# Moving one early load to the GpSimd queue and one attention wave by one item in a lightning-attention and MLP kernel

## The chip, the core and the metric

The kernel runs on one core of a Trainium2 chip. A core has a tensor engine (PE) with its own weight loads (PEld), a vector engine (DVE), a scalar engine (ACT), GpSimd (POOL) and a sync engine (SP). They run side by side, each in its own program order, and wait for one another by semaphores. SP and POOL also issue the transfers between device memory and on-chip memory: SP's go through hardware queue q1, POOL's through software queue q0. The metric is the device time of one execution in microseconds (us); less is better.

## The reference

Linear attention with decay over 4 batches, 8 heads, 768 positions and head size 64, in blocks of 64 positions. Its output, laid out as 3072 tokens of 512 values, goes through an MLP with 2048 hidden values and the activation h · sigmoid(1.702 h).

```python
for b in range(nb):                                   # blocks of 64 positions
    intra = einsum('bhic,bhjc->bhij', qb, kb) * Dmask  # decay lam**(i-j), causal
    intra = einsum('bhij,bhjd->bhid', intra, vb)
    inter = einsum('bhid,bhde->bhie', qb * lam_pow, kv_state)
    out[:, :, sl] = intra + inter
    kv_state = lam_block * kv_state + einsum('bhsd,bhse->bhde', kb * rev_pow, vb)

x = out.transpose(0, 2, 1, 3).reshape(B * S, H * D)   # 3072 x 512
h = x @ w_in                                          # 512 -> 2048
g = h * (1.0 / (1.0 + exp(-1.702 * h)))
y = g @ w_out                                         # 2048 -> 512
```

## The kernel before, in words

**Waves.** The work is cut into six waves of 512 tokens. Waves 0 and 1 are of one kind: each holds two *halves* (c = 0, 1), and a half is the first 256 positions of one batch, two positions to a partition. Half c of wave w is batch 2w + c. Waves 2 to 5 hold 128 positions of all four batches each. The code calls c "batch" within a wave; "v of wave 0's batch 1" is `load_one(0, 1, "v", v)`.

**Attention of a half.** `do_cast` multiplies k and q by their decay powers and casts them to bf16 (on DVE or POOL); `turn_pe` transposes them on PE, and ACT or DVE copies the transposes out; `cast_v` casts v to bf16; `d_scores` makes the scores on PE and the masks on DVE; `d_one` and `d_state` make the state on PE from k and v; `d_out` multiplies masked scores with v, and `d_inter` adds the part from the state; `d_x` copies the result out as `xT`, the MLP's input. For wave 1 `start(1, c)` holds the scores and the first state, `end(1, c)` the outputs and the copies to `xT`. Waves 2 to 5 use `turn_dma`, a transpose by transfer issued on SP, and the functions `n_scores` to `n_out`.

**The MLP** is cut into items. `mlp1(w, fc)` is four matmuls of 512 columns (L393) with the activation on ACT; `mlp1_half(w, c, fc)` does two values of fc for the 256 columns of one half (eight matmuls of 256 columns, L405), so it needs only that half's `xT`. `mlp2(w, g, j)` is four matmuls of the second layer (L417), and the last of each g copies to `o_sb` on DVE (L421) and stores.

**The order is written out by hand.** The block from L457 to L512 is wave 0's start: casts, transposes, scores, outputs of its half 0, and the beginning of half 1. Between them stand *fillers* (`fill`, L143): matmuls on zeros whose result nobody reads. From L545 on, a main list holds all MLP items of all waves, and a side list holds attention steps, each with a place on the main list: a step at place n + 24 is issued just before main item 24 of that wave. `mlp_items` makes wave 0's list (31 items, indices 0 to 30: three half items, twelve `mlp1`, sixteen `mlp2`), and wave 1's starts at index 31. Because engines run in program order, a step that waits holds up all later instructions of its engine.

**The loads.** `load(0)` at L104 issues on SP k, q, v of half 0 (in two transfers each), then k and q of half 1 (two each), then v of half 1 in one transfer of 512 KB: eleven in all. The weights go through POOL and are converted from f32 to bf16 on the way: `w_in` in five parts (parts 0 and 1 of 256 KB, the others of 512 KB as written), `w_out` in four parts of 512 KB. POOL's order is: wait for v of half 0 (`gate_pool`, L472), issue w_in part 0, cast k of half 1 (four instructions, L198), issue w_in parts 1 and 2, cast half of v of half 1 (L211), issue w_in parts 3 and 4 and the four parts of w_out. SP's next instruction after `load(0)` is `gate_sync` (L506), a tiny transfer that reads w_out part 1; so SP issues `load(1)` only when that part has landed. Then come `load(2)`, the four transposes of wave 2 and the stores of wave 0.

**Where v of half 1 is used.** `cast_v(0, 1, (act_copy, pool_copy))` (L499) casts one part on ACT, one on POOL; then PE's `d_one(0, 1)` (L510) and `d_out` in `end(0, 1)` read it. On PE, `mlp1_half(0, 0, 0)` (L509), the first use of the weights, stands just ahead of `d_one(0, 1)`.

Of the kernel before, what the change touches and what calls it, by code (L numbers as in the profile page):

```python
# [24 lines left out]
def kernel(  # L25
# [13 lines left out]
    nc = tc.nc  # L39
# [36 lines left out]
    def load_one(w, c, nm, src):  # L76
        x = ld.tile([P, H, 2 * D], f32, tag=f"{nm}{c}", name=f"{nm}f")
        if w < ND:
            n = H if w or (nm == "v" and c) else H // 2
            for h in range(0, H, n):  # L80
                nc.sync.dma_start(  # L81
                    out=x[:, h : h + n],
                    in_=src[2 * w + c, h : h + n, 0 : 2 * P, :].rearrange("h (s a) d -> s h (a d)", a=2))
        else:
            nc.sync.dma_start(out=x.rearrange("p h (a d) -> p (h a) d", a=2),
                              in_=src[2 * c : 2 * c + 2, :, w * P : (w + 1) * P, :].rearrange("b h s d -> s (b h) d"))
        loaded[w, c, nm] = x

    def load(w, nms="kqv"):
        src = {"k": k, "q": q, "v": v}  # L90
        if w < ND:
            for c in range(HF):
                for nm in nms:
                    load_one(w, c, nm, src[nm])
        else:
            for nm in nms:
                for c in range(HF):
                    load_one(w, c, nm, src[nm])
# [3 lines left out]
    ones = const.tile([1, P], f32)  # L102
    nc.vector.memset(ones, 1.0)
    load(0)  # L104

    nc.scalar.preload_act_table_set("natural_log_exp_and_others")
# [29 lines left out]
    def acc(name, dt=f32, shape=None, tag="a"):  # L136
        return ps.tile(shape or [P, 4, P], dt, tag=tag, bufs={"a": 5, "mm": 3}[tag], name=name)

    def fill(n, new=None):
        if new:  # L140
            fill_ps[0] = acc("ps_fill", shape=[P, W], tag=new)
        for _ in range(n):
            nc.tensor.matmul(fill_ps[0], zero[:, 0:P], zero, start=True, stop=True)  # L143
# [31 lines left out]
    def load_w_in(j):  # L175
        c0 = sum(IN_CH[:j]) * P
        nc.gpsimd.dma_start(
            out=w_in_sb[j], in_=moe_w_in.rearrange("(kc ki) f -> ki kc f", ki=P)[:, :, c0 : c0 + IN_CH[j] * P])
# [10 lines left out]
    def do_cast(w, c, nm, eng, g=None):  # L189
        if g in (None, 0):  # L190
            cast[w, c, nm] = work.tile([P, 2, HD], bf16, tag=f"{nm}s{c}", name=f"{nm}s")
        f, x = loaded[w, c, nm], cast[w, c, nm]
        if w < ND:
            pw = {"k": kd_pow, "q": qd_pow}[nm]
            for R in (0, 1) if g is None else (g,):
                for j in range(2):
                    h = slice(4 * R + 2 * j, 4 * R + 2 * j + 2)
                    eng.tensor_tensor(x.rearrange("p a (r i j d) -> p r j i a d", i=2, j=2, d=D)[:, R, j],  # L198
                                      f[:, h].rearrange("p i (a d) -> p i a d", a=2),
                                      pw[:, h].unsqueeze(3).to_broadcast([P, 2, 2, D]), op=MUL)  # L200
        else:
            pw = {"k": k_pow, "q": q_pow}[nm]
            n = 2 * H // 4
            for j in range(2):
                eng.tensor_tensor(x.rearrange("p b (r i j d) -> p j (b r) i d", i=2, j=2, d=D)[:, j],  # L205
                                  f.rearrange("p h (a d) -> p (h a) d", a=2).rearrange("p (n j i) d -> p j n i d", j=2, i=2)[:, j],
                                  pw.rearrange("p b (r j i) -> p j (b r) i", i=2, j=2)[:, j].unsqueeze(3).to_broadcast([P, n, 2, D]),
                                  op=MUL)
# [19 lines left out]
    def turn_pe(w, c, nm, copy=act_copy, g=None):  # L228
        x = cast[w, c, nm]
        rr = list(range(NP)) if g is None else [2 * g, 2 * g + 1]  # L230
        t = acc("ps_t", bf16, [P, len(rr), 2, P])
        for i, r in enumerate(rr):
            for a in range(2):
                nc.tensor.transpose(t[:, i, a, :], x[:, a, r * P : (r + 1) * P], ident)  # L234
        if g in (None, 0):
            trans[w, c, nm] = work.tile([P, 2 * NP, P], bf16, tag=f"{nm}T{c}", name=f"{nm}T")
        copy(trans[w, c, nm][:, 2 * rr[0] : 2 * rr[0] + 2 * len(rr)], t.rearrange("p r a s -> p (r a) s"))
# [195 lines left out]

    def mlp_items(w):
        if w < ND:
            f = 4 if w == 0 else 8
            items = [(mlp1_half, w, c, fc) for c in range(HF) for fc in range(0, f, 2) if w or c or fc]
            items += [(mlp1, w, fc) for fc in range(f, FFC)]
        else:
            items = [(mlp1, w, fc) for fc in range(FFC)]  # L440
        if w == 0:
            items += [(mlp2, w, g, j) for j in range(NCH) for g in range(3)]
            return items + [(mlp2, w, 3, j) for j in range(NCH)]
        items += [(mlp2, w, g, j) for g in range(G) for j in range(NCH)]
        if w == NW - 1:
            items = items[:-NCH]
            for c0, c1 in ((0, 256), (256, 384), (384, 512)):
                items += [(mlp2, w, G - 1, j, c0, c1) for j in range(NCH)]
        return items

    def gate_pool(x):
        nc.gpsimd.tensor_copy(behind_q, x)
# [4 lines left out]
    with tc.manual_schedule():  # L457
# [4 lines left out]
            nc.scalar.activation(blk_pow[rows].rearrange("p (r i) -> p r i", i=2),  # L462
                                 ln_lam[rows].rearrange("p (r j i) -> p r j i", i=2, j=2)[:, :, j, :], EXP, scale=1.0 * P)
        nc.scalar.activation(warm, q_pow[:, 0, 0:1], GELU)
        fill(5)
        for nm, copies in (("k", (dve_copy, act_copy)), ("q", (act_copy, dve_copy))):
            for g in range(2):
                do_cast(0, 0, nm, nc.vector, g)
            for g in range(2):
                turn_pe(0, 0, nm, copies[g], g)  # L470
                fill(2 if nm == "k" or g == 0 else 0)
        gate_pool(loaded[0, 0, "v"][0:1, 0, 0:1])  # L472
        load_w_in(0)
        cast_v(0, 0, (act_copy, act_copy))
        d_scores(0, 0, 0)
        fill(1)
        d_scores(0, 0, 1)
        fill(3)
        for g in range(2):
            do_cast(0, 1, "k", nc.gpsimd, g)  # L480
        for j in (1, 2):
            load_w_in(j)
        d_one(0, 0, "mm")
# [18 lines left out]
        for j in range(NCH):  # L502
            load_w_out(j)
        nc.gpsimd.affine_select(mask, mask, pattern=[[0, 1], [1, P]], channel_multiplier=-1, base=0,
                                compare_op=mybir.AluOpType.is_ge, fill=0.0)
        gate_sync(w_out_sb[1][0:1, 0, 0:2])  # L506
        load(1)
        d_scores(0, 1, 1, True)
        mlp1_half(0, 0, 0)  # L509
# [36 lines left out]
        for w in range(NW):  # L546
            n = len(main)
            main += mlp_items(w)
            e = len(main)
            x = w + 1  # L550
            if x < ND:
                for c, (k_at, q_at, v_at, k_turn, q_turn, s_at, e_at) in enumerate(
                        ((19, 20, 19, 24, 25.5, 27, 30), (26.5, 28, 28, 29, 30, 32, 34))):
                    side += [(n + k_at, (do_cast, x, c, "k", (nc.vector, nc.gpsimd)[c])),
                             (n + q_at, (do_cast, x, c, "q", nc.vector)),
                             (n + v_at, (cast_v, x, c, ((pool_copy, pool_copy), (act_copy, act_copy))[c])),
                             (n + k_turn, (turn_pe, x, c, "k", act_copy)),
                             (n + q_turn, (turn_pe, x, c, "q", act_copy)),
                             (n + s_at, (start, x, c)), (n + e_at, (end, x, c))]
            elif x < NW:  # L560
                for c in range(HF):
                    tk, tq = (n + 2.1 + 2 * c, n + 4 + c) if x == ND else (n + 4 + 2 * c, n + 5 + 2 * c)
                    side += [(tk, (do_cast, x, c, "k", nc.vector)), (tk, (turn_dma, x, c, "k")),
                             (tq, (do_cast, x, c, "q", nc.vector)), (tq, (turn_dma, x, c, "q")),
                             (n + 10 + 2 * c, (cast_v, x, c, (dve_copy,)))]
                if x == ND:
                    side += [(n + 7, (stores,))]
                t = n + 16
                side += [(t, (n_two, x, 0)), (t + 4, (n_two, x, 1)), (t + 9, (n_rest, x))]
            if w + 2 < NW:  # L570
                side += [(n + (12 if w else 20), (load, w + 2))]
# [36 lines left out]
```

## Time and profile before

| | us |
|---|---|
| six runs | 207.19, 208.25, 208.55, 209.45, 209.83, 209.97 |
| median | 209.0 |
| the profiled execution | 209.97 |
| its span in the profile | 208.2 |

All times below are from the start of that span. The transfers of the first 45 us, from the profile's transfer lists and the chain of waits:

| transfer | issued on | issued at | landed at |
|---|---|---|---|
| k of half 0, two parts | SP | 0.81, 1.33 | 3.6, 4.2 |
| q of half 0, two parts | SP | 1.85, 2.40 | 6.4, 6.9 |
| v of half 0, two parts | SP | 2.95, 3.50 | 7.9, 8.6 |
| k of half 1, two parts | SP | 4.16, 5.59 | 9.9, 11.3 |
| q of half 1, two parts | SP | 6.32, 7.01 | 11.3, 12.1 |
| v of half 1 | SP | 7.97 | 16.60 |
| w_in part 0 | POOL | 8.26 | 16.29 |
| w_in part 1 | POOL | 12.23 | 17.9 |
| w_in part 2 | POOL | 12.98 | 21.7 |
| w_in parts 3, 4 | POOL | 17.2, 18.0 | 24.7, 27.3 |
| w_out parts 0, 1 | POOL | 18.7, 19.4 | 30.0, 32.53 |
| k, q, v of wave 1, half 0 | SP | 33.35, 33.78, 34.40 | 39.16, 40.7, 42.2 |

What PE did at those places: 5.83 first transposes of half 0; 9.10 and 9.77 its two score groups; 10.87 `d_one(0, 0)`; 11.24 first transposes of half 1; 14.97 end of half 1's scores; 16.30 `mlp1_half(0, 0, 0)`; 17.29 `d_one(0, 1)`; 19.38 main item 0; 22.06 first use of w_in part 2; 32.42 first `mlp2`; 40.0 to 40.2 the transposes of wave 1's k; 50.7 wave 1's first MLP item; 66.67 scores of wave 2; 205.3 last matmul.

How to read the profile: a line of the timeline gives the start, the length, the engine, the source line, the operation with output and inputs, how many instructions it merges, and in brackets how long the engine was idle before it and what it then waited for. A line of the chain of waits gives the start, the length and what held up the chain there. A row of busy time gives the sum, the share of the span and the number of instructions.

### The profile page before, as it was taken

Reading aid. Unit: us, or ns where it says so; the run is one execution under the profiler, and the core shown is the slowest. Engines: PE = TensorE matmul, PEld = TensorE weight load, DVE = VectorE, ACT = ScalarE, POOL = GpSimd, SP = SyncE. Lnnn points to the kernel's source line nnn. Section 1 sums busy time; section 2 is a strip of 40 time slices with the busy share of each in tenths; the row PEclk is TensorE's granted clock in tenths of the full one; section 3 lists DMA queues with packets and bytes.
Section 4 is the critical chain, followed back from the end, with each engine's and each line's share of the span. In section 5 each row is a group of like instructions: output and inputs, shape, how many; then the busy total and the mean of one; then the engine's idle time right before and its main releaser. Section 6 shows DMA issues by size and latency. Waiting matters only on the chain.

```text
span 208.2 us, 4271 instructions
## 1 busy us (share of the span) xinstructions
PE 199.5 (96%) x1806; PEld 105.3 (51%) x1830; DVE 89.4 (43%) x160; ACT 86.3 (41%) x158; POOL 16.4 (8%) x37
## 2 busy tenths in 40 slices
PE   7988999999999999999999999999999999999994
PEld 2556544457864454444464444464444454444453
DVE  1793000486970844750744750744750741100121
ACT  4866662148666012466012466012466012566000
POOL 4368200060000000000000000000000000000000
PEclk9999999999999999999999999999999999999999
DMA  5999999999999899989992379991360021100112
GB/s 150 328 221 155 184 202 219 284 324 228 231 210 163 199 247 231 263 193 211 212 257 104 93 167 213 238 252 52 99 154 3 14 90 50 50 0 0 54 50 101
DMA packets 87640, 33.82 MB, mean 162 GB/s; under 512 B 67398, under 2 KB 84678, under 8 KB 87622
## 3 DMA queue, kind: packets, MB, share of 16 engines
q1 hardware_dynamic: 82868, 29.37, 56.7%
q0 software_dynamic: 4752, 4.19, 13.0%
q8 instruction: 14, 0.23, 0.4%
q14 instruction: 4, 0.03, 0.0%
q10 hardware_dynamic: 2, 0.00, 0.0%
HBM read 27.26 MB, written 6.29 MB: 161 GB/s over the span
## 4 chain that ended last, share of the span: by engine, by line
PE 75%; DMA 15%; SPq 4%; DVE 2%; POOL 1%; issue 1%
PE ps_out L417 35%; PE ps_h L393 28%; DMA w_out<-in_moe_w_out_dram 6%; DMA vf<-in_v_dram 4%; PE ps_h L405 3%; SPq L81 3%; DMA kf<-in_k_dram 3%; PE ps_s L331 2%; DMA qT<-qs 2%; PE ps_o L381 2%; PE ps_o L368 1%; DVE o_sb L421 1%; PE ps_t L234 1%; PE ps_kv L355 1%; DVE ks L198 1%
## 5 line engine op out<-in xcount | busy, mean ns | idle before, releaser
L417 PE MATMUL ps_out<-w_out,g_sb 128*128 128x512 bf16 (+2 forms) x400 | 83.8, 362 | 1.1 <-issue 0.6
L393 PE MATMUL ps_h<-xT,w_in 128*128 128x512 bf16 x330 | 73.2, 379 | 0.3
L395 ACT ACTIVATE g_sb<-ps_h 128x512 bf16<-128x512 f32 x84 | 50.2, 597 | 45.2 <-PE ps_h L393 45.2
L417 PEld LDWEIGHTS <-g_sb 128*128 128x128 bf16 x416 | 38.2, 98 | 41.0
L393 PEld LDWEIGHTS <-w_in 128*128 128x128 bf16 x336 | 32.9, 98 | 39.2
L421 DVE COPY o_sb<-ps_out 128x512 f32<-128x512 f32 (+2 forms) x26 | 16.9, 650 | 52.4 <-PE ps_out L417 52.3
L339 DVE SCALAR_TENSOR_TENSOR sm<-ps_s,inv_pow,mask 128x512 bf16<-128x512 f32 x32 | 21.8, 743 | 28.1 <-PE ps_s L331 28.1
L385 ACT CAST xT<-ps_o 128x512 bf16<-128x512 f32 x16 | 8.2, 599 | 38.3 <-PE ps_o L381 38.3
L405 PE MATMUL ps_h<-xT,w_in 128*128 128x256 bf16 x96 | 11.4, 273 | 1.3 <-DMA w_in<-in_moe_w_in_dram 1.3
L198 DVE TENSOR_TENSOR ks<-kf,kd_pow 128x256 bf16<-128x256 f32 x8 | 2.9, 421 | 22.2 <-DMA kf<-in_k_dram 18.9
L405 PEld LDWEIGHTS <-w_in 128*128 128x128 bf16 x96 | 9.0, 98 | 3.1 <-DMA w_in<-in_moe_w_in_dram 1.5
L205 DVE TENSOR_TENSOR qs<-qf,q_pow 128x512 bf16<-128x512 f32 x16 | 10.3, 685 | 0.0
L205 DVE TENSOR_TENSOR ks<-kf,k_pow 128x512 bf16<-128x512 f32 x16 | 10.3, 684 | 0.0
L263 DVE TENSOR_TENSOR sm<-ps_s,mask_d 128x512 bf16<-128x512 f32 x14 | 8.8, 684 | 0.8 <-PE ps_s L255 0.5
L407 ACT ACTIVATE g_sb<-ps_h 128x512 bf16<-128x512 f32 x12 | 7.2, 598 | 4.3 <-PE ps_h L405 4.3
L143 PE MATMUL ps_fill<-zero 128*128 128x512 bf16 x18 | 7.3, 536 | 1.4 <-DVE zero L113 1.4
L359 DVE SCALAR_TENSOR_TENSOR kv<-kv,blk_pow,ps_kv 128x256 bf16<-128x256 bf16 x12 | 5.0, 475 | 6.0 <-PE ps_kv L355 6.0
L217 ACT COPY kT<-ps_t 128x512 bf16<-128x512 bf16 (+1 forms) x4 | 3.2, 797 | 8.4 <-PE ps_t L234 8.4
L198 DVE TENSOR_TENSOR qs<-qf,qd_pow 128x256 bf16<-128x256 f32 x16 | 5.8, 425 | 0.1
L214 DVE CAST v_sb<-vf 128x1024 bf16<-128x1024 f32 x8 | 5.2, 687 | 0.8 <-DMA vf<-in_v_dram 0.8
L331 PEld LDWEIGHTS <-kT 64*128 64x128 bf16 x128 | 3.6, 94 | 3.9 <-issue 3.9
L331 PE MATMUL ps_s<-qT,kT 64*128 64x128 bf16 x128 | 5.1, 217 | 0.3 <-DMA qT<-qs 0.3
(68 smaller groups left out, 91.9 us busy)
## 6 DMA issues: line engine op xcount, KB each, us to landing
vf<-in_v_dram SPq DMA_DIRECT2D x11, 512.0 KB, 6.8
kf<-in_k_dram SPq DMA_DIRECT2D x10, 512.0 KB, 5.7
qf<-in_q_dram SPq DMA_DIRECT2D x10, 512.0 KB, 6.9
out_dram<-o_sb SPq DMA_DIRECT2D x15, 256.0 KB, 2.0
out_dram<-o_sb SPq DMA_DIRECT2D x17, 128.0 KB, 2.4
w_out<-in_moe_w_out_dram POOLq DMA_DIRECT2D x4, 512.0 KB, 14.0
w_in<-in_moe_w_in_dram POOLq DMA_DIRECT2D x3, 512.0 KB, 8.7
kf<-in_k_dram SPq DMA_DIRECT2D x4, 256.0 KB, 3.0
```

What stands on the lines that cost most here:

```text
L143: nc.tensor.matmul(fill_ps[0], zero[:, 0:P], zero, start=True, stop=True)
L198: eng.tensor_tensor(x.rearrange("p a (r i j d) -> p r j i a d", i=2, j=2, d=D)[:, R, j], f[:, h].rearrange("p i (a d) -> p i a d", a=2), p ...
L205: eng.tensor_tensor(x.rearrange("p b (r i j d) -> p j (b r) i d", i=2, j=2, d=D)[:, j], f.rearrange("p h (a d) -> p (h a) d", a=2).rearran ...
L263: nc.vector.tensor_tensor(sm.rearrange("p i a s -> p i (a s)"), flat, mask_d.rearrange("p o a b s -> p o (a b s)").to_broadcast([P, 2, 2 * ...
L331: nc.tensor.matmul(s2[h][:, b, :], kT[hs, (b % 2) * NP + p, :], qT[hs, (b % 2) * NP + p, :], start=True, stop=True)
L339: nc.vector.scalar_tensor_tensor(sm, s, inv_pow[:, n : n + 1], mask.to_broadcast([P, B, P]), op0=MUL, op1=MUL)
L385: nc.scalar.copy(xT[w][:, p, :], ps_o.rearrange("p b s -> p (b s)"))
L393: nc.tensor.matmul(h, w_in_sb[j][:, kc, i * P : (i + 1) * P], xT[w][:, kc, :], start=(kc == 0), stop=(kc == KC - 1))
L395: nc.scalar.activation(g_of[w][:, fc, :], h, GELU)
L405: nc.tensor.matmul(h[:, u, :], w_in_sb[j][:, kc, i * P : (i + 1) * P], xT[w][:, kc, cols], start=(kc == 0), stop=(kc == KC - 1))
L417: nc.tensor.matmul(ps_out, g_of[w][:, fc, g * P : (g + 1) * P], w_out_sb[j][:, fc % CW, c0:c1], start=(fc == 0), stop=(fc == FFC - 1))
L421: nc.vector.tensor_copy(o, ps_out)
```

## The change

1. `load_one` issues v of wave 0's half 1 on POOL (`nc.gpsimd`), and `load(0)` leaves it out. It is issued where the new line `load_one(0, 1, "v", v)` stands, in POOL's order behind w_in part 0 and the four casts of k, ahead of w_in parts 1 and 2.
2. Five fillers go: the first group has three for five; behind the four transpose groups stand 2, 1, 1, 0 for 2, 2, 2, 0; and the one between the two score groups is taken out.
3. All of wave 1's attention steps stand one main item later.
4. Wave 1's list of MLP items begins with five half items for each half (fc 0 to 9), then six `mlp1`; before it was four and eight.

```diff
@@ load_one
-                nc.sync.dma_start(
+                (nc.gpsimd if w == 0 and c and nm == "v" else nc.sync).dma_start(
@@ load
-                    load_one(w, c, nm, src[nm])
+                    if w or c == 0 or nm != "v":
+                        load_one(w, c, nm, src[nm])
@@ mlp_items
-            f = 4 if w == 0 else 8
+            f = 4 if w == 0 else 10
@@ start of wave 0
-        fill(5)
+        fill(3)
...
                 turn_pe(0, 0, nm, copies[g], g)
-                fill(2 if nm == "k" or g == 0 else 0)
+                fill(2 - g if nm == "k" else 1 - g)
...
         d_scores(0, 0, 0)
-        fill(1)
         d_scores(0, 0, 1)
         fill(3)
         for g in range(2):
             do_cast(0, 1, "k", nc.gpsimd, g)
+        load_one(0, 1, "v", v)
         for j in (1, 2):
             load_w_in(j)
@@ side list of wave 1
                 for c, (k_at, q_at, v_at, k_turn, q_turn, s_at, e_at) in enumerate(
-                        ((19, 20, 19, 24, 25.5, 27, 30), (26.5, 28, 28, 29, 30, 32, 34))):
+                        ((20, 21, 20, 25, 26.5, 28, 31), (27.5, 29, 29, 30, 31, 33, 35))):
```

## The prediction, made before the changed kernel was run

> **What bounds the kernel now.** I read the page first: PE is busy 199.5 of 208.2 us, so the gaps on PE are 8.7 us in all. Two of the page's lines show how little else is near the limit.
>
> ```profile
> PE 199.5 (96%) x1806; PEld 105.3 (51%) x1830; DVE 89.4 (43%) x160; ACT 86.3 (41%) x158; POOL 16.4 (8%) x37
> PEclk9999999999999999999999999999999999999999
> ```
>
> The gaps lie almost wholly in the first 20 us, and the waits list gives PE only two of any size after its first instruction. The chain of waits, in order of time, then shows something that PE's business hides: up to 39 us, and once more at 67 us, a chain of transfers sets the pace.
>
> ```profile
> 7.97 8.62 DMA vf<-in_v_dram
> 16.60 0.06 issue
> 16.66 0.61 POOL v_sb L211
> 17.26 1.44 POOL w_in L177 x2
> 18.70 0.72 POOL w_out L181
> 19.42 13.09 DMA w_out<-in_moe_w_out_dram
> 32.53 0.77 SPq L455
> 33.35 5.81 DMA kf<-in_k_dram
> 39.19 1.45 DVE ks L198 x4
> ...
> 62.90 4.38 DMA qT<-qs
> 67.31 0.51 PE ps_s L331 x12
> ```
>
> SP has nothing to do until w_out's second part lands at 32.53 (its longest wait, 23.3 us); from 33.35 it issues loads of waves 1 and 2 without a gap until 57.4, then four transposes. The last lands at 67.28, and PE has waited for it since 66.96. So there are two clocks: PE's own work, and the transfers through w_out's gate. They meet at 67.3 with PE 0.35 us ahead. Behind that point PE waits for nothing but 0.05 to 0.2 us of issue. **A gain before 67.3 reaches the end only if both clocks gain.**
>
> The timeline gives the place that the change touches:
>
> ```profile
> 9.96 2.32 POOL L198 TENSOR_TENSOR ks<-kf,kd_pow 128x256 bf16<-128x256 f32 x4 [0.76 <-DMA kf<-in_k_dram]
> 12.23 1.55 POOL L177 DMA_DIRECT2D w_in<-in_moe_w_in_dram  x2
> 16.30 1.05 PE L405 MATMUL ps_h<-xT,w_in 128*128 128x256 bf16 x8 [1.33 <-DMA w_in<-in_moe_w_in_dram]
> 16.62 0.62 ACT L217 CAST v_sb<-vf 128x512 bf16<-128x512 f32 x1 [1.37 <-DMA vf<-in_v_dram]
> 16.66 0.61 POOL L211 CAST v_sb<-vf 128x512 bf16<-128x512 f32 x1 [2.87 <-DMA vf<-in_v_dram]
> 67.31 0.51 PE L331 MATMUL ps_s<-qT,kT 64*128 64x128 bf16 x12 [0.35 <-DMA qT<-qs]
> ```
>
> PE waits 1.33 us for the first weights (landed 16.29), and v of batch 1 lands only 0.31 us later (16.60). Behind v stand both casts, then PE's d_one at 17.29.
>
> [...] from 12.5 to 13.0 us POOL's queue moved 96 packets and SP's 100. So moving v takes no byte away; it only changes the order. [...] fillers come 0.43 us apart to 7 us and 0.21 us later. [...] the w_in issues at 12.23 beside DVE's casts took 0.75 us, the w_out issues beside an idle DVE 0.77.
>
> **The change, part by part.**
>
> *Fillers.* Five of twenty go. Two of the first five end at 5.4 instead of 5.83; the first cast halves are ready at 4.63 + 2 x 0.36 = 5.35, so transposes start 0.4 us earlier. The rest brings the second scores from 9.77 to about 9.15 (they then wait for qT). But the next transposes, at 11.24, need POOL's first two casts, done at 9.96 + 2 x 0.61 = 11.17: up to there the gain is zero. Behind it DVE's masks end 0.46 us earlier, and the scores of batch 1 end near 14.5 instead of 14.97. All this only makes the wait for weights or v longer: worth 0 at the end. [...]
>
> *First weights.* They are issued at 8.26 in both kernels. By half microseconds POOL's queue moves its first packets at 11.0 to 11.5, when SP's k and q of batch 1 run out (2.62 MB at some 330 GB/s). Without v beside them, 528 packets at 166 a half microsecond (14.5 to 15.0, nearly alone) take 1.6 us: they land at 13.5 to 14.5 instead of 16.29. PE starts them at 14.5, not 16.30.
>
> *v of batch 1.* Now issued on POOL behind its four casts, at 12.28 instead of SP's 7.97. Until the first packet: w_in's fourth part was issued at 17.21 and its packets came at about 19.2, so 2.0 us; between 1.2 (the queue was already busy) and 2.7 [...]. Transfer: 1,024 packets at SP's 345 a half microsecond are 1.5 us, at w_in's 166 they are 3.1; I take 1.8, nearer to SP's[...]. End of landing: 0.4 us (k's first halves, with no backlog, 0.3 to 0.5). Sum: 12.28 + 2.0 + 1.8 + 0.4 = **16.5**, bounds 15.4 and 18.6. Before it was 16.60. So PE gains **0.1 us** (bounds +1.2 and -2.0) at d_one; the wait of 1.33 us for weights becomes one for v. Queued behind v: on ACT the copy of a score tile (0.58) and on DVE its mask (0.43), which hold PE's d_out, as before; on POOL all of w_in's last parts and w_out.
>
> *Weights behind v.* w_in's second part is issued up to 1.5 us later and runs behind v: 16.1 + 1.6 + a tail of 0.5 to 1.2 = 18.2 to 18.9, needed at 19.3: covered. The third: 2.65 us more, 21 to 22, needed at 22: just covered, up to 0.3 us exposed. [...]
>
> *The gate.* Before, POOL's queue nearly ran dry at 18.0 to 20.0: 81, 39, 50 and 78 packets a half microsecond where 98 is usual, 144 missing, 0.73 us. With v in the same queue two weight parts still stand in line when POOL goes on, so that dip goes; a new one opens between the first weights' end (12.9) and v's first packet (14.3), 1.4 us. The mean loses 0.7, but landings came 2.0 us behind the mean (third w_in: mean 19.6, landed 21.7), and an idle 1.4 us lets the laggards catch up. I take 32.53 - 0.3, bounds -1.2 and +1.5.
>
> *One item later, half-wave items.* No work is added but two pairs as halves: 16 matmuls at 0.112 us (L405, 40 in 4.47) for 8 at 0.220 (L393, 41 in 9.01), +0.03 us. Wave 1's transposes stand 0.87 us later in PE's order (four L417 matmuls), so PE comes at 40.77 and finds k cast (40.3): the 0.27 us wait there goes. All other steps of wave 1 get 0.87 us more slack. One cover goes: the last output item no longer lies between end(1,0) and the first half-wave item, and its o_sb copy (0.69) now precedes the xT copy on DVE. DVE ends xT about 1.75 us after d_out begins, PE's d_out, states and eight transposes take 1.7: 0 to 0.15 us, I take 0.1. Wave 2's casts follow 0.8 us later on DVE; SP took them 1.7 to 3.1 us after they were ready, so nothing waits.
>
> *Sum.* PE reaches the scores of wave 2 at 66.96 - 0.1 + 0.03 + 0.1 = 67.0; qT lands at 67.28 - 0.3 = 67.0. So PE goes on 0.3 us earlier. The profiled execution took 209.97 us (span 208.2 and 1.8 around it) and becomes 209.7; it was the slowest of six, so against the median, 209.0, I forecast **208.7**.
>
> **Rivals.** *Both clocks gain:* POOL's queue starts v at once and runs at SP's rate: v 15.4, gate -1.2. PE would be 1.2 + 0.35 - 0.13 = 1.4 us earlier, transfers 1.2: 207.8. For it: the queue is busy when v is issued; against: w_in's first part needed 3 us. *Only one gains:* v lands at 15.5, but the gate stays; PE stands 1.3 us longer at the wave-2 scores: 209.0. For it: SP's gapless chain. This holds too if v merely changes places with the weights, so that the change does not do what it says. *Slower:* v, late on POOL's queue. Its price is one for one once v lands later than 16.60 + 0.35 - 0.13 = 16.8, the point where PE falls behind qT. At 18.6 PE is 1.8 us late: 210.8; PE then idles from 15.5 to 19.3[...]. [...]
>
> **How the numbers follow.** Forecast 0.45, its own range 208.2 to 209.2; both clocks gain 0.13; only one 0.17; slower 0.25, of which somewhat under half passes 1%. One per cent (2.1 us) is about what a measurement can tell here, as the runs of before differ by 2.8. Faster by over 1% needs more than the best bounds give and is left 0.05; slower by over 1% gets 0.11; within 0.84. Range 207.5 to 210.6.
>
> **What would show it.** First weights landed by 14.5 and no PE wait for them; a PE wait for v_sb instead; v issued near 12.3 and landed by 16.8; no dip of POOL's packets at 18 to 20; w_out's gate at 31.3 to 33; PE waiting under 0.2 us at wave 1's transposes; the wave-2 scores within 0.5 us of 67. Wrong: v past 17.5, L405 matmuls at twice their length, or a new wait for w_in.

## The result, and the profile after

The changed kernel took 210.39 us (median of 35 runs, 208.88 to 212.53) where the kernel before, run beside it, took 208.35 (72 runs, 206.96 to 212.07). The ratio is 1.0087, with a 95% interval of 1.0066 to 1.0107: slower, by more than the measurement is uncertain. Ratios here leave out the executions that lie over 1.5% above the fastest of their kernel, so they are not the plain quotients of the medians. The forecast had been a small gain, 209.0 to 208.7.

The profiled execution took 209.47 us, span 207.8; the profiled execution before 209.97, span 208.2. Profile against profile, the change gained 0.5 us (forecast: 0.3), while the medians lost 2.0. Most of what follows is about that contradiction.

From the page of the changed kernel, the row of busy time and the row of POOL's DMA queue (packets, MB, share of 16 engines):

```profile
PE 198.4 (95%) x1811; PEld 105.1 (51%) x1833; DVE 89.5 (43%) x160; ACT 86.3 (42%) x158; POOL 17.1 (8%) x38
q0 software_dynamic: 4896, 4.72, 14.1%
```

PE is busy 198.4 of 207.8 us, so the gaps are now 9.4 us (8.7 before). v moved to POOL's queue adds only 144 packets and 0.53 MB to the 4,752 and 4.19 MB before: v's packets there carry about 4 KB each, and are not the 1,024 small ones of my estimate.

The waits of PE (total, times, longest):

```profile
PE ps_kv L276 <- ACT v_sb L218: 1.5, 1, 1.5
```

The wait for the first weights has gone, and the one for v stands in its place (1.5 us for 1.33). The chain of waits shows the same (start, length, what held it):

```profile
4.17 5.57 DMA kf<-in_k_dram
9.89 2.27 POOL ks L199 x4
12.16 4.48 DMA vf<-in_v_dram
...
19.49 2.77 PE ps_h L406 x24
```

v is now behind POOL's four casts: they end at 12.16, v takes 4.48 us from there, and behind its landing PE is the chain up to the end. The gate of w_out and the transfers of wave 1 have left the chain. From the timeline:

```profile
12.16 0.95 POOL L81 DMA_DIRECT2D vf<-in_v_dram  x1
14.82 1.05 PE L406 MATMUL ps_h<-xT,w_in 128*128 128x256 bf16 x8
16.70 0.61 POOL L212 CAST v_sb<-vf 128x512 bf16<-128x512 f32 x1 [2.08 <-DMA vf<-in_v_dram]
17.34 0.38 PE L276 MATMUL ps_kv<-v_sb,ks 64*64 64x64 bf16 x13 [1.47 <-ACT v_sb L218]
19.42 2.84 PE L406 MATMUL ps_h<-xT,w_in 128*128 128x256 bf16 x24
66.54 0.74 PE L332 MATMUL ps_s<-qT,kT 64*128 64x128 bf16 x16
```

PE starts the first weights at 14.82 without a wait, ends them at 15.87 and stands until 17.34. d_one(0, 1) and main item 0 begin at 17.34 and 19.42: the same places as in the profile before (17.29, 19.38). So against that profile nothing is lost; the question is what that profile stands for.

### The profile page after: what moved, and what is told of

The parts are those of the page before. It is cut to its first block, busy times and chain, and to the rows that moved or that the text cites. A ratio compares the mean times of both kernels' runs of the same rounds, so it can differ in the third digit from the quotient of the medians.

```text
span 207.8 us, 4280 instructions
## 1 busy us (share of the span) xinstructions
PE 198.4 (95%) x1811; PEld 105.1 (51%) x1833; DVE 89.5 (43%) x160; ACT 86.3 (42%) x158; POOL 17.1 (8%) x38
## 4 chain that ended last, share of the span: by engine, by line
PE 88%; DMA 5%; SPq 1%; DVE 1%; issue 1%; POOL 1%; ACT 1%; ACTq 0%; POOLq 0%
PE ps_out L418 39%; PE ps_h L394 34%; PE ps_h L406 6%; DMA kf<-in_k_dram 3%; PE ps_s L332 2%; DMA vf<-in_v_dram 2%; PE ps_o L382 2%; SPq L81 1%; PE ps_o L369 1%; DVE o_sb L422 1%; POOL ks L199 1%; PE ps_t L235 1%; PE ps_o L313 1%; PE ps_kv L356 1%; PE ps_o L295 1%
## 5 line engine op out<-in xcount | busy, mean ns | idle before, releaser
L394 PE MATMUL ps_h<-xT,w_in 128*128 128x512 bf16 x322 | 71.5, 379 | 0.3
L394 PEld LDWEIGHTS <-w_in 128*128 128x128 bf16 x328 | 32.1, 98 | 38.2
L406 PE MATMUL ps_h<-xT,w_in 128*128 128x256 bf16 x112 | 13.1, 273 | 0.0
L199 DVE TENSOR_TENSOR ks<-kf,kd_pow 128x256 bf16<-128x256 f32 x8 | 2.9, 420 | 22.6 <-DMA kf<-in_k_dram 19.3
L406 PEld LDWEIGHTS <-w_in 128*128 128x128 bf16 x112 | 10.5, 98 | 1.7 <-DVE xT L215 0.2
L144 PE MATMUL ps_fill<-zero 128*128 128x512 bf16 x14 | 6.1, 539 | 1.5 <-DVE zero L114 1.4
```

The costliest lines, as they stand in the source:

```text
L394: nc.tensor.matmul(h, w_in_sb[j][:, kc, i * P : (i + 1) * P], xT[w][:, kc, :], start=(kc == 0), stop=(kc == KC - 1))
L406: nc.tensor.matmul(h[:, u, :], w_in_sb[j][:, kc, i * P : (i + 1) * P], xT[w][:, kc, cols], start=(kc == 0), stop=(kc == KC - 1))
```

## The experiments

The expectations weigh three theories. *Late v*: v lands later than it mostly does on SP, and PE waits for it. *Clock*: the changed kernel falls more often into a short stretch at half the TensorE clock. Of its executions 16 have a mean clock of 0.992, over spans of about 209 us; at half clock that is a stretch of 3.3 us, worth 1.7 (an estimate from these clocks). The one profile that shows such a stretch (e9) has 3.4 us of it, at 0.50. *Order*: wave 1's new order costs time.

Each row was timed beside the kernel before on the same chip. The last column counts timed executions whose mean granted TensorE clock was below 0.995.

| Run | Median us | Ratio, 95% | Below 0.995 |
|---|---|---|---|
| kernel before, again | 208.01 | 0.9995 [0.9966, 1.0024] | 6 of 22 |
| changed kernel | 210.39 | 1.0087 [1.0066, 1.0107] | 21 of 36 |
| v alone (e1) | 210.03 | 1.0073 [1.0047, 1.0100] | 6 of 17 |
| fewer fillers alone (e2) | 208.60 | 1.0009 [0.9984, 1.0034] | 0 of 22 |
| wave 1's order alone (e7) | 208.20 | 0.9981 [0.9957, 1.0004] | 1 of 22 |
| all but v's move (e6) | 208.06 | 1.0001 [0.9973, 1.0028] | 0 of 22 |
| changed, six fillers in the wait (e3) | 209.23 | 1.0052 [1.0032, 1.0072] | 0 of 22 |
| changed, four fewer fillers (e8) | 209.99 | 1.0078 [1.0052, 1.0104] | 12 of 20 |
| changed, v ahead of the casts (e5) | 208.53 | 0.9997 [0.9967, 1.0027] | 1 of 14 |
| before, v ahead of the casts, wave 1's order (e10) | 208.79 | 1.0002 [0.9979, 1.0025] | 0 of 22 |

The changed kernel's 36 are its 35 timed executions and the profiled one. The kernel before itself was below 0.995 in 19 of 164 executions beside these runs.

### The kernel before, again

No edit.

> The kernel before, once more, for the granted clock and the span of each execution, which are known for the changed kernel only: there 15 executions at clock 0.998 to 1.0 had a median of 209.28 us, 17 at 0.991 to 0.992 had 210.82, and 4 at 0.984 had 212.21. Clock theory (what is lost is a stretch of about 3.4 us at half clock, worth some 1.6 us, that the changed kernel falls into more often): before shows the same steps, but most executions at 1.0, with the 207.5 us that are its commonest time belonging to 1.0. Order theory (wave 1's new order costs time at full clock): before at clock 1.0 is 1 to 2 us faster than the changed kernel at 1.0. Late-v theory: the clock is the same in both, and the times differ without it.

The profiled execution took 207.8 us, 2.2 less than the profile that I had predicted from. Its timeline (SPq is SP's DMA issue):

```profile
7.94 0.69 SPq L81 DMA_DIRECT2D vf<-in_v_dram  x1
14.19 0.61 POOL L211 CAST v_sb<-vf 128x512 bf16<-128x512 f32 x1 [0.91 <-DMA vf<-in_v_dram]
14.76 1.05 PE L405 MATMUL ps_h<-xT,w_in 128*128 128x256 bf16 x8 [0.30 <-ACT sm L261]
15.73 0.37 PE L275 MATMUL ps_kv<-v_sb,ks 64*64 64x64 bf16 x12
17.68 2.84 PE L405 MATMUL ps_h<-xT,w_in 128*128 128x256 bf16 x24
30.89 0.77 SPq L455 DMA_DIRECT2D behind<-w_out  x1
65.04 0.62 PE L331 MATMUL ps_s<-qT,kT 64*128 64x128 bf16 x16
```

Here v, issued at 7.94 for 7.97, lands before 14.2, and not at 16.60; the first weights cost no wait for a transfer either. Everything behind it is earlier: d_one(0, 1) at 15.73, not 17.29; the gate at 30.89, not 32.53; wave 2's scores at 65.04 with no wait for qT, not 66.67 with one of 0.35 us. The changed kernel's 66.54, which has no wait either, is 0.1 ahead of the one profile of before (0.5 with its wait) and 1.5 behind the other.

The windows show where the changed kernel is late. The columns are the stretch, its length, the busy times of PE, PEld, DVE, ACT and POOL, then granted clock, DMA share and GB/s. This run of the kernel before:

```profile
12.00:15.00 3.00, 2.57 (x56) 1.62 (x53) 2.70 (x8) 2.39 (x5) 2.09 (x4) 1.00 1.34 196
15.00:18.00 3.00, 2.78 (x83) 2.14 (x81) 1.36 (x4) 2.66 (x8) 3.00 (x5) 1.00 1.26 173
```

The same windows of the changed kernel:

```profile
12.00:15.00 3.00, 2.85 (x79) 1.94 (x70) 2.70 (x7) 2.27 (x6) 2.62 (x4) 1.00 0.66 88
15.00:18.00 3.00, 1.53 (x48) 1.27 (x47) 1.44 (x4) 1.52 (x4) 1.30 (x3) 1.00 1.18 242
```

From 12 to 15 us the changed kernel moves 88 GB/s where the kernel before moves 196: the DMA share is 0.66 for 1.34, and v has only just been issued (12.16). From 15 to 18 it moves more, but PE's busy time falls from 2.78 to 1.53 us.

### One part at a time: v alone, fewer fillers alone

```diff
@@ e1, from the kernel before: load_one, load and the new line, as in the change
+        load_one(0, 1, "v", v)
```

> Only v of half 1 moved to POOL's queue behind w_in part 0; all twenty fillers and wave 1's order as before. Clock theory: with the fillers kept, PE is busier in the first 10 us, so fewer stretches at half clock than in the whole change; ratio 0.998 to 1.004. Late-v theory: v alone carries the loss, ratio 1.007 to 1.011, with v landing past 17 us in the profile. Order theory: ratio 0.997 to 1.001.

```diff
@@ e2, from the kernel before
-        fill(5)
+        fill(3)
...
-                fill(2 if nm == "k" or g == 0 else 0)
+                fill(2 - g if nm == "k" else 1 - g)
...
-        fill(1)
```

> Only the five fillers taken out; v on SP and wave 1's order as before. Clock theory: this alone carries most of the loss, ratio 1.006 to 1.010, with more executions at clock 0.992 than the kernel before has. Late-v and order theory: no loss, 0.998 to 1.002, as the fillers stand in time in which PE waits for POOL's casts or for weights.

v alone gives 1.0073, nearly the whole 1.0087; the fillers alone give 1.0009, with no execution below 0.995. At a clock of 0.995 or more v alone has a median of 209.68 and the kernel before beside it 208.12, so its loss is mostly lateness; its 6 of 17 below 0.995 can't be told from the 6 of 22 of the kernel before in the same series. The waits of PE in the run with v alone:

```profile
PE ps_kv L276 <- ACT v_sb L218: 0.9, 1, 0.9
PE ps_h L394 <- DMA w_in<-in_moe_w_in_dram: 0.7, 1, 0.7
PE ps_s L332 <- DMA qT<-qs: 0.3, 1, 0.3
```

In this profile v is cast a little earlier (16.31 for 16.67) and PE, with all twenty fillers, comes to it a little later, so the wait for v is 0.9 and not 1.5; part of the loss appears as a wait for the weights behind v (0.7), which I had bounded at 0.3. The theory that the missing fillers carry the loss by themselves fell. Whether they make a dip of the clock likelier once v is late (21 of 36 against 6 of 17) is not separated by these runs.

### All but v's move, and wave 1's order alone

```diff
@@ e7, from the kernel before (e6: the same and e2's edit)
-            f = 4 if w == 0 else 8
+            f = 4 if w == 0 else 10
...
-                        ((19, 20, 19, 24, 25.5, 27, 30), (26.5, 28, 28, 29, 30, 32, 34))):
+                        ((20, 21, 20, 25, 26.5, 28, 31), (27.5, 29, 29, 30, 31, 33, 35))):
```

> Fewer fillers and wave 1's new order with its five half-wave items, but v of half 1 on SP as before. Late-v theory: the loss goes, ratio 0.996 to 1.002, v landing at 14 to 16.6 us. Order theory: the loss stays, 1.005 or more. Clock theory: about as many spells of half clock as with the fillers alone (none in 22), as PE does not wait 1.5 us for v.

> Only wave 1's attention one item later and five half-wave items; v on SP and all fillers. Order theory: ratio 1.004 to 1.01, with new waits on PE between 40 and 60 us. Late-v theory: no loss, 0.996 to 1.001; a gain where PE otherwise stands waiting for wave 1's k, at most 0.4 us.

0.9981 and 1.0001, both intervals with 1 in them: the other parts of the change are worth nothing that can be measured, together or in wave 1 alone. The loss is v's.

### v on the same queue, but ahead of the casts

```diff
@@ e5, from the changed kernel
         load_w_in(0)
+        load_one(0, 1, "v", v)
...
             do_cast(0, 1, "k", nc.gpsimd, g)
-        load_one(0, 1, "v", v)
```

> The whole change, but v of half 1 is issued on POOL directly behind w_in part 0, ahead of the four casts of k: at about 9.0 us instead of 12.2. Late-v theory (v lands about 4.5 us after its issue on POOL, and that issue is late because it stands behind the casts, while on SP it mostly lands at 14.2): v lands at 14 to 15.3 us, d_one follows by 16, ratio 0.996 to 1.001. If POOL's queue itself is what makes v late (its packets wait for w_in part 0 and go slower), v still lands past 16 and the ratio stays 1.005 to 1.009. The casts of k begin up to 1 us later, which may take back 0.3 us.

The ratio is 0.9997. The timeline:

```profile
9.03 0.91 POOL L81 DMA_DIRECT2D vf<-in_v_dram  x1
9.96 2.33 POOL L199 TENSOR_TENSOR ks<-kf,kd_pow 128x256 bf16<-128x256 f32 x4
14.67 0.61 POOL L212 CAST v_sb<-vf 128x512 bf16<-128x512 f32 x1 [0.89 <-DMA vf<-in_v_dram]
15.88 0.37 PE L276 MATMUL ps_kv<-v_sb,ks 64*64 64x64 bf16 x12
65.22 0.62 PE L332 MATMUL ps_s<-qT,kT 64*128 64x128 bf16 x16
```

v is issued at 9.03 and not 12.16, lands before 14.67, and the casts still begin at 9.96. d_one and wave 2's scores are back within 0.2 us of the run of the kernel before at 207.8. So neither POOL's queue nor its large packets cost the time; the place behind the casts does.

### The clock: fillers in the wait, fewer fillers, more profiles

```diff
@@ e3, from the changed kernel, between mlp1_half(0, 0, 0) and d_one(0, 1)
+        fill(6)
```

> The whole change, and six fillers more on PE between the first half item and d_one of half 1, in the 1.5 us in which PE waits for v. Clock theory: the idle stretch at 15.8 to 17.3 goes, clock 1.0 in most executions, ratio to before 0.995 to 1.002. [...] Late-v and order theory: no help, 1.007 to 1.011.

Each filler adds one matmul on zeros, whose result nothing reads. The timeline:

```profile
14.64 1.05 PE L406 MATMUL ps_h<-xT,w_in 128*128 128x256 bf16 x8
15.53 1.46 PE L144 MATMUL ps_fill<-zero 128*128 128x512 bf16 x6
16.40 0.62 ACT L218 CAST v_sb<-vf 128x512 bf16<-128x512 f32 x1 [1.40 <-DMA vf<-in_v_dram]
17.07 0.44 PE L276 MATMUL ps_kv<-v_sb,ks 64*64 64x64 bf16 x16
19.16 2.84 PE L406 MATMUL ps_h<-xT,w_in 128*128 128x256 bf16 x24
```

PE works through the wait, and d_one begins when v is cast, neither earlier nor later than without the fillers (0.67 us behind the start of the cast, in both). Yet the median falls from 210.39 to 209.23, and no execution of 22 is below 0.995. That is the median of the changed kernel's own executions at a clock of 0.995 or more (209.28), so the ratio that is left, 1.0052, is v's lateness. Both theories were partly right: the clock carries a part, v's landing the other.

> The changed kernel, one more look. About six in ten of its executions have a granted clock of 0.984 to 0.992, none of which the profile at hand shows. If this look meets one, clock theory says: the L406 and L394 matmuls, or the small ones before them, follow each other at twice their distance for about 3.4 us, in a stretch that begins within 4 us behind the wait for v at 15.8 to 17.3, and the span is 208.7 to 209.5. If the stretch lies elsewhere (beyond 60 us, or before 11 us), the wait for v is not its cause.

No edit; another profile, to catch the clock falling. It took 209.74 us at a clock of 0.998 and didn't show it (v landed early for this kernel, 15.87, and PE waited 0.6 for it, 0.57 for w_in part 2 and 0.28 for wave 2's qT). On the clock this decided nothing; it shows that v's landing alone doesn't set the time, as the first profile, with v 0.8 us later, took 209.47.

```diff
@@ e8, from the changed kernel
-        fill(3)
...
-            fill(1, "a")
```

> The whole change, and four fillers more taken out (three ahead of d_one(0, 0), one ahead of half 1's scores), so that PE does less between 9 and 17 us while v is waited for. Clock theory: still more spells of half clock, at least 8 in 10 executions at 0.992 or 0.984, ratio 1.010 or more, and the profile likely shows one: twice the usual distance between matmuls for about 3.4 us, beginning between 16 and 22 us. If the wait for v is not the cause of the spells, their share stays near 21 in 36 and the ratio at 1.007 to 1.010.

12 of 20 executions below 0.995, against 21 of 36: no more than in the changed kernel. I had expected eight in ten, and a ratio of at least 1.010; it was 1.0078. Four fillers fewer ahead of the wait did not raise the share.

> The changed kernel, a third look, as the two so far met no spell of half clock. Where it meets one, clock theory expects it to begin between 16 and 22 us and to last about 3.4 us, and v's landing at 16 to 17 us with a wait of PE of 0.6 to 1.6 us ahead of it.

This profile, without an edit again, took 211.21 us, at a mean clock of 0.992, and shows what such an execution loses. Its timeline on PE, then its windows (stretch, length, PE busy, granted clock, DMA share, GB/s):

```profile
17.57 0.38 PE L276 MATMUL ps_kv<-v_sb,ks 64*64 64x64 bf16 x13 [1.52 <-ACT v_sb L218]
...
19.66 4.46 PE L406 MATMUL ps_h<-xT,w_in 128*128 128x256 bf16 x24
23.95 6.42 PE L394 MATMUL ps_h<-xT,w_in 128*128 128x512 bf16 x29
```

```profile
16.00:18.00 2.00, 0.48 (x32) 1.00 1.30 180
18.00:20.00 2.00, 1.78 (x59) 0.98 1.19 191
20.00:22.00 2.00, 2.00 (x12) 0.50 1.14 146
22.00:24.00 2.00, 2.00 (x14) 0.66 1.21 189
24.00:26.00 2.00, 2.00 (x12) 1.00 1.26 206
```

PE waits 1.52 us, about as in the first profile; but then the 24 matmuls of main item 0 take 4.46 us instead of 2.84, so 1.6 us are lost. At half clock in the dip (0.50), the shares 0.98, 0.50 and 0.66 of two microseconds each make 0.08 + 2.0 + 1.36 = 3.4 us of half clock, which costs 1.7 us. The page's row of the granted clock has one 7 among 39 nines: easily overlooked.

This is the one profile that shows such a dip. Waits as long (1.47 in the first profile, 1.64 with four fewer fillers) passed without one. Of the 21 executions below 0.995, 17 have a mean clock of 0.991 or 0.992, as this one has, and four 0.984, which would be two such stretches (an estimate from this profile). That their stretches also belong to the wait for v is concluded from the six fillers inside it, with which none of 22 executions was below 0.995; where the second stretch of the four lies is open, and so is what decides which executions are hit.

### An attempt at a better version

```diff
@@ e10, from the kernel before: e7's edit, load_one and load as in the change, and
         load_w_in(0)
+        load_one(0, 1, "v", v)
```

> v of half 1 on POOL ahead of the casts as in the run before last, wave 1's new order with five half-wave items, and all twenty fillers as in the kernel before: the parts of which none showed a loss. Late-v and clock theory: no loss, ratio 0.996 to 1.000, at most 1 in 10 executions below clock 0.995. If it is under 0.998 with its interval below 1, this version is better than both kernels.

1.0002. In this profile the cast of v began at 15.48. No version here beats the kernel before beyond its interval; wave 1's order alone (0.9981) comes nearest, and its interval touches 1.

## Why the prediction was wrong

**The step that failed** is a sentence of *v of batch 1*: "Before it was 16.60. So PE gains 0.1 us". The landing in the changed kernel was right (16.5 forecast; cast at 16.67), but what it was compared with was one execution. In five profiles of kernels with v on SP, the POOL cast that follows v's landing began at 16.66, 14.19, 15.98, 14.87 and 14.37; in six with v behind the casts at 16.70, 16.34, 16.43, 15.87, 16.72 and 16.94. The base was the latest of five, and it came from the slowest of six runs (209.97; the fastest was 207.19), which I had noted and corrected only by a shift of the total. The correction assumed that the lost 1 or 2 us lay elsewhere. Most of them lay at this very place: between the two profiles of the kernel before, 2.2 us apart, d_one(0, 1) differs by 1.56 and main item 0 by 1.70. The first weights, which v was to stop delaying, were late in that profile too: PE began them at 16.30 there and at 14.76, 15.51, 14.67 and 15.20 in the other four with v on SP. So there was mostly little for the change to save, and v's later landing was left. The sum also put the clock behind the wait for v at nothing.

**What came in its place** has two terms. v's lateness: executions of the changed kernel at a clock of 0.995 or more have a median of 209.28, those of the kernel before beside the experiments 208.2, so 1.1 us. The profiles agree roughly: d_one(0, 1) begins at 16.3 on average in the five with v on SP (15.64 to 17.29) and at 17.1 in the six with v behind the casts (16.50 to 17.57). The clock: over all its executions the changed kernel has 210.39, 1.1 more, while for the kernel before the same step is 0.25 (208.45). These two terms only divide the measured loss, so it proves nothing that they add up to about its 2.04. What tests them are the runs: fillers in the wait take the clock's part away and leave 1.0052, that is 1.1 us, and v ahead of the casts takes away both (0.9997).

**The rival "slower"** had the right mechanism, v late on POOL's queue and one for one behind that. One of its terms was mis-sized. Its point of 16.8, "where PE falls behind qT", came from the same execution; in the run at 207.8 us PE didn't wait for qT at all. There d_one begins at 15.73, and from the start of v's cast to d_one the changed kernel takes 0.67 (16.67 to 17.34), so by this estimate v may land up to 15.06 for nothing and costs one for one behind that: 1.6 us at 16.67. Three of the five landings on SP are ahead of that point, all six behind the casts are past it. The clock behind such a wait cost 1.6 us in the profile that shows it, and the wait was one of 1.52, where this rival has PE idle from 15.5 to 19.3.

The rivals in which one clock or both gain didn't come: v gained nothing and the gate came later.

Point by point, the rest:

- *Fillers*: worth 0 was right (e2: 1.0009).
- *First weights*: forecast to land 13.5 to 14.5 and PE at 14.5; PE began at 14.82 with no wait for them.
- *v's transfer*: the parts were wrong and made up for one another. The issue took 0.95 us, and the first packets of 4 KB came between 13.5 and 14.0, 1.3 to 1.8 us behind the issue (2.0 forecast); from there to the cast it took about 3 (2.2 forecast), 4.5 in all. Six profiles show 4.4 to 4.8 us from issue to cast, and the changed kernel with v ahead of the casts (e5), behind w_in part 0 in the queue, 5.6.
- *Weights behind v*: 0 in the profile after, but 0.57 and 0.7 in two others, beyond the 0.3 that I allowed. v's move is not the only cause: with wave 1's order alone, v on SP and cast at 14.37, PE waited 0.99 for the same part, and that profile took 209.31.
- *The gate*: forecast 32.23; it was issued at 32.96, within the bounds, but later than before. It didn't matter: PE came to wave 2's scores at 66.54 and found qT there. The dip of POOL's packets did go (93 and 97 a half microsecond from 18.5 to 19.5, for 39 and 50), but the run of the kernel before at 207.8 doesn't have it either (99 and 107): once more it belonged to the one profile.
- *Wave 1's order*: 0.27 us of wait did go (the transposes of k at 41.09 follow PE's own work), and the whole was worth nothing measurable (e7), as forecast.

Why v on SP lands anywhere from 14.2 to 16.6 is seen but not explained. In the run at 207.8 us SP's queue ran at 326 to 350 packets a half microsecond from 9.0 to 11.5, and POOL's packets hardly began before 12 (26 from 11.5 on); in the profile at 209.97 POOL's began at 11.0 to 11.5, and from 12 to 13.5 the two took turns at 95 to 101 each, with v still in line. What makes them take turns earlier wasn't tried.

## What to carry to other kernels

A landing time in one profile is a sample: where an argument rests on one transfer having been late, look at a second execution of the unchanged kernel first, the more so if the profiled run is the slowest of those shown. The load that was moved to another queue here was worth what its place in that queue gave: a ratio of 0.9997 issued ahead of POOL's casts, 1.0087 behind them; so try such a load ahead of that engine's compute first. A wait of 1.52 us on PE was followed by 1.6 us lost to the clock, in the one profile that shows it. Six filler matmuls inside the wait took that price away (0 of 22 executions below 0.995, for 21 of 36), while four fewer ahead of it did not raise the share (12 of 20).

## What the runs showed of the hardware that was not expected

- With POOL's queue nearly empty, v still came slowly at first in the changed kernel. By half microseconds its queue moved 9 packets (0.04 MB) at 13.5 and 8 (0.03 MB) at 14.0, and only at 15.0 and 15.5 46 and 65 (0.19 and 0.18 MB). Issued ahead of the casts, 60 packets (0.18 MB) went in one half microsecond at 12.5. Why the first ones take so long is open.
- The same fp32 rows go as 1,024 small packets from SP and as some 128 of 4 KB from POOL (144 more packets in POOL's row and 1,040 fewer in SP's, for 0.52 MB).
- In the one profile that shows it, the clock fell to 0.50 at 19.9 us (by the windows), more than 2 us after PE had gone back to work at 17.57, so main item 0 lost the time (4.46 us for 2.84) and not the small matmuls right behind the wait.
